# Four column groups instead of two for a one-row output on TensorE, with two casts and a store from four partitions

## The chip, the cores and the metric

The kernel runs on one core of a Trainium2 chip. The metric is the device time of one execution in microseconds (us). The five runs of the kernel before agree within 0.12%. A profile covers one execution; its span, from the first to the last instruction, is about 1.8 us shorter than the time in the kernel before. Engines: PE is TensorE (PEld its weight loads), DVE is VectorE, ACT is ScalarE, SP issues the loads and the store. PSUM is the memory in which PE sums up its products. The granted clock is the share of full speed that the profile shows for PE: 1.00 is called full clock here, 0.50 half clock.

## The reference, cut to what matters

One token of 576 numbers goes through windowed attention over a key and value cache (32 query heads, 16 key and value heads, the last 4096 positions) and through a two-layer GELU network. A gate mixes the two.

```python
x = A_x                                               # [1, 1, 576]
g = _sigmoid((x * gate_w).sum(-1, keepdims=True))
a = _A_ref(x, A_k_cache, A_v_cache, A_wq, A_wo)       # ... attention, then o @ wo, wo is [4096, 576]
b = _B_ref(x, B_w1, B_b1, B_w2, B_b2)                 # gelu(x @ w1 + b1) @ w2 + b2, w2 is [4608, 576]
return g * a + (1 - g) * b
```

Nearly all the work is reading 53.6 MB of caches and weights once. The output is a single row of 576 numbers. It is the sum of 68 products of a 128-vector with a 128 x 576 block: 36 blocks of w2, 32 of wo, all added up in PSUM. The gate is already in the vectors.

## The kernel before: the parts that matter

The row is kept as two halves of 288 columns, on PSUM partitions 0 and 32 and in different banks. Every block takes two matmuls with one stationary column each.

```python
    y_ps = ps_y.tile([64, 1024], FP32, name="y_ps")
    y_out = (y_ps[0:1, 0:DH], y_ps[32:33, 512 : 512 + DH])      # DH = 288

    def y_add(vec, row, start=False, stop=False):
        for s in range(2):
            nc.tensor.matmul(y_out[s], lhsT=vec, rhs=row[:, s * DH : (s + 1) * DH],
                             start=start, stop=stop, skip_group_check=True)
```

`y_add` is used in the middle of the kernel (first half of w2, 18 blocks) and at its end (32 blocks of wo, 18 of w2), in the order in which the last loads land. Loads are all issued by SP, far ahead of their use.

```python
    for r0, r1 in ((0, 16), (16, RO)):                           # RO = 32
        nc.sync.dma_start(out=wo_t[:, r0:r1, :], in_=wo_src[:, r0:r1, :])
    for j0, j1 in ((0, 10), (10, 16), (16, 18)):                 # the last three loads
        nc.sync.dma_start(out=w2_t[:, NJ + j0 : NJ + j1, :], in_=w2_src[:, 1, j0:j1, :])
    # ... (attention output to ov) ...
    for r in range(RO):
        y_add(ov[:, r : r + 1], wo_t[:, r, :])
    for f in range(NJ, NF):
        y_add(gt[:, f : f + 1], w2_t[:, f, :], stop=(f == NF - 1))
    out_row = const.tile([1, D], BF16, name="out_row")
    nc.scalar.copy(out=out_row[:, DH:D], in_=y_out[1])
    nc.vector.tensor_copy(out=out_row[:, 0:DH], in_=y_out[0])
    nc.sync.dma_start(out=out.rearrange("a b d -> (a b) d"), in_=out_row[:])
```

## Time and profile before

| | before |
|---|---|
| time, median of 5 runs | 134.01 us (133.95 to 134.11) |
| span of the profiled run | 132.1 us |
| 864 KB piece of w2 landed (last but one load) | 128.21 us |
| last `y_ps` matmuls | 128.25 to 129.44 us |
| casts | 129.43 to 129.88 us |
| store issued | 129.94 us |
| end | 132.1 us |

First the page of the kernel before: busy time of PE in us with its share of the span and its instructions, then the granted clock of PE and the busy share of the 16 DMA engines, in tenths, in 40 slices of the span.

```profile
PE 77.4 (59%) x1126; PEld 51.1 (39%) x1126; DVE 55.4 (42%) x80; ACT 12.9 (10%) x25; POOL 0.7 (1%) x6
...
PEclk9999999999999999999999996555555555556998
DMA  7999998999999999999999999999999999999960
```

The DMA engines are busy nearly to the end and PE is not: the loads bound the kernel. PE's clock falls to half near 80 us and comes back in the last tenth of the span.

The end of the chain of waits, before (start, length, what):

```profile
100.84 27.37 DMA w_t<-in_B_w_dram
128.21 0.04 issue
128.25 1.19 PE y_ps L193 x16
129.44 0.44 DVE out_row L437
```

After the landing at 128.21 us only the last matmuls, a cast and the store remain. The chain names the 864 KB piece; the very last one, 288 KB for two blocks, landed at 128.94 us by its semaphore, while PE was at work on the other six.

Instructions of the kernel before in order of time (start, length, engine, line, what, count, and in brackets the wait before):

```profile
72.97 1.14 PE L193 MATMUL y_ps<-w_t,gt 128*1 128x288 bf16 x15
...
117.16 4.00 PE L193 MATMUL y_ps<-wo_t,ov 128*1 128x288 bf16 x32 [3.04 <-DMA wo_t<-in_A_wo_dram]
...
122.67 2.12 PE L193 MATMUL y_ps<-wo_t,ov 128*1 128x288 bf16 x32 [1.51 <-DMA wo_t<-in_A_wo_dram]
...
128.25 1.15 PE L193 MATMUL y_ps<-w_t,gt 128*1 128x288 bf16 x16 [0.73 <-DMA w_t<-in_B_w_dram]
...
129.43 0.45 DVE L437 CAST out_row<-y_ps 1x288 bf16<-1x288 f32 x1 [15.09 <-PE y_ps L193]
129.46 0.39 ACT L436 CAST out_row<-y_ps 1x288 bf16<-1x288 f32 x1 [42.24 <-PE y_ps L193]
129.94 0.31 SPq L438 DMA_DIRECT2D out_dram<-out_row  x1
```

The groups at 117.16 and 122.67 have the same 32 matmuls, 4.00 us at half clock and 2.12 us at full clock. The casts on DVE and ACT run side by side.

The stretches of the same run (us, then busy time of PE, PEld, DVE, ACT and POOL, granted clock, DMA share, GB/s):

```profile
117.00:119.00 2.00, 1.84 (x16) 1.00 (x17) 0.00 (x0) 0.00 (x0) 0.00 (x0) 0.50 0.97 415
128.20:129.40 1.20, 1.15 (x16) 0.62 (x15) 0.00 (x0) 0.00 (x0) 0.00 (x0) 1.00 0.09 27
```

The clock is 0.50 at 117 us and 1.00 in the tail.

And the DMA queues in the stretch 117.0 to 127.8 us (queue and kind, then packets, MB and the share of the 16 engines' time):

```profile
q1 hardware_dynamic: 492, 4.24, 93.7%
```

In the last 11 us of the load stage there is one queue only, that of the loads.

### The profile page before, as it was taken

The page shows a single profiled execution, that of the slowest core. Times are in us where ns is not written, and L with a number is a line of the kernel's source. Part 1 is how long each engine was busy: PE and PEld are TensorE (multiplying, and loading weights), DVE is VectorE, ACT ScalarE, POOL GpSimd, SP SyncE. Part 2 cuts the span into 40 slices and gives each one's busy share as a digit, 9 for nine tenths or more (in the row PEclk, how much of TensorE's full clock was granted, in tenths as well). Part 3 has the DMA queues.
Part 4 walks back from the last instruction along what each step waited for, and adds up shares of the span by engine and source line. Part 5 has one row for each costly group of instructions (what it writes and reads, how often), then busy time and mean ns, then how long its engine had stood idle before and what let it go on. Part 6 is the DMA issues. An engine that isn't in the chain of part 4 may idle for free.

```text
span 132.1 us, 2458 instructions
## 1 busy us (share of the span) xinstructions
PE 77.4 (59%) x1126; PEld 51.1 (39%) x1126; DVE 55.4 (42%) x80; ACT 12.9 (10%) x25; POOL 0.7 (1%) x6
## 2 busy tenths in 40 slices
PE   0038999084699769769779460007942952456651
PEld 0035999084234323223223230007942952333430
DVE  6059100503978988988985710653000000100001
ACT  3000000003000000000000059940000000000001
POOL 2000000000000000000000000000000000000000
PEclk9999999999999999999999996555555555556998
DMA  7999998999999999999999999999999999999960
GB/s 246 421 443 411 448 518 368 398 427 427 427 417 432 422 431 419 427 436 417 454 408 442 451 446 417 407 466 427 397 451 387 431 417 428 429 407 427 406 249 0
DMA packets 3190, 53.78 MB, mean 407 GB/s; under 512 B 358, under 2 KB 362, under 8 KB 620
## 3 DMA queue, kind: packets, MB, share of 16 engines
q1 hardware_dynamic: 3170, 53.61, 95.7%
q8 instruction: 9, 0.15, 0.4%
q10 hardware_dynamic: 10, 0.01, 0.0%
q14 instruction: 1, 0.01, 0.0%
HBM read 53.62 MB, written 0.00 MB: 406 GB/s over the span
## 4 chain that ended last, share of the span: by engine, by line
DMA 67%; PE 12%; DVE 8%; ACT 7%; issue 2%; SPq 1%; DVEq 0%
DMA k_t<-in_A_k_cache_dram 26%; DMA w_t<-in_B_w_dram 21%; DMA wq_t<-in_A_wq_dram 20%; ACT p_t L351 7%; PE o_ps L402 5%; DVE kt L300 3%; PE q_ps L257 3%; DVE pt L359 2%; DVE m L321 2%; PE s_ps L309 1%; PE y_ps L193 1%; SPq L415 1%; PE t_ps L377 0%; DVE out_row L437 0%; SPq L417 0%
## 5 line engine op out<-in xcount | busy, mean ns | idle before, releaser
L300 DVE STREAM_TRANSPOSE kt<-k_t 128x2048 f32<-128x2048 f32 x16 | 36.0, 2290 | 9.7 <-DMA k_t<-in_A_k_cache_dram 9.7
L309 PE MATMUL s_ps<-kt,qz_flat 128*128 128x512 bf16 x128 | 32.3, 399 | 9.2 <-DVE kt L300 9.2
L309 PEld LDWEIGHTS <-qz_flat 128*128 128x128 bf16 x128 | 12.8, 100 | 28.3 <-issue 14.7
L402 PE MATMUL o_ps<-pt,v_t 128*128 128x8 bf16 x512 | 14.6, 168 | 8.5 <-DMA v_t<-in_A_v_cache_dram 6.5
L402 PEld LDWEIGHTS <-v_t 128*128 128x128 bf16 x512 | 14.3, 104 | 8.9 <-DMA v_t<-in_A_v_cache_dram 6.7
L351 ACT ACTIVATE p_t<-s_ps,negm 128x512 bf16<-128x512 f32 x8 | 9.7, 1412 | 44.9 <-DVE negm L342 44.9
L219 PE MATMUL h_ps<-x,w_t 128*128 128x2 bf16 x162 | 10.2, 202 | 0.0
L219 PEld LDWEIGHTS <-w_t 128*128 128x128 bf16 x162 | 10.1, 169 | 0.0
L420 DVE TENSOR_TENSOR om<-o_ps,rgh 128x128 bf16<-128x128 f32 x1 | 0.3, 292 | 22.2 <-PE o_ps L402 22.2
L193 PE MATMUL y_ps<-wo_t,ov 128*1 128x288 bf16 x64 | 6.1, 364 | 4.6 <-DMA wo_t<-in_A_wo_dram 4.6
L359 DVE STREAM_TRANSPOSE pt<-p_t 128x2048 bf16<-128x2048 bf16 x2 | 4.6, 2312 | 7.4 <-ACT p_t L351 7.4
L377 PE MATMUL t_ps<-ls,ones 128*128 128x32 f32 x2 | 0.6, 396 | 11.9 <-DVE ls L375 11.9
L193 PE MATMUL y_ps<-w_t,gt 128*1 128x288 bf16 x72 | 5.6, 285 | 2.1 <-DMA w_t<-in_B_w_dram 2.1
L437 DVE CAST out_row<-y_ps 1x288 bf16<-1x288 f32 x1 | 0.4, 446 | 15.1 <-PE y_ps L193 15.1
L257 PE MATMUL q_ps<-x,wq_t 128*128 128x2 bf16 x144 | 4.0, 166 | 4.0 <-DMA wq_t<-in_A_wq_dram 4.0
L193 PEld LDWEIGHTS <-ov 128*1 128x1 bf16 x64 | 3.4, 103 | 7.0 <-issue 4.5
L257 PEld LDWEIGHTS <-wq_t 128*128 128x128 bf16 x144 | 3.9, 104 | 4.0 <-DMA wq_t<-in_A_wq_dram 4.0
L377 PEld LDWEIGHTS t_ps<-ls,ones 128*128 128x128 f32 x2 | 0.5, 310 | 12.2 <-issue 12.2
L120 PE MATMUL xs_ps<-one_b,rows 1*128 1x1 bf16 x9 | 0.7, 195 | 7.2 <-DVE rows L117 7.2
L193 PEld LDWEIGHTS <-gt 128*1 128x1 bf16 x72 | 3.2, 83 | 3.9 <-issue 2.9
L436 ACT CAST out_row<-y_ps 1x288 bf16<-1x288 f32 x1 | 0.4, 390 | 42.2 <-PE y_ps L193 42.2
L228 DVE COPY hacc<-h_ps 128x36 f32<-128x36 f32 x1 | 0.2, 196 | 9.4 <-PE h_ps L219 9.4
(68 smaller groups left out, 28.7 us busy)
## 6 DMA issues: line engine op xcount, KB each, us to landing
k_t<-in_A_k_cache_dram SPq DMA_DIRECT2D x8, 2048.0 KB, 32.3
v_t<-in_A_v_cache_dram SPq DMA_DIRECT2D x3, 4096.0 KB, 29.8
wq_t<-in_A_wq_dram SPq DMA_DIRECT2D x1, 4608.0 KB, 25.8
wo_t<-in_A_wo_dram SPq DMA_DIRECT2D x2, 2304.0 KB, 20.2
v_t<-in_A_v_cache_dram SPq DMA_DIRECT2D x2, 2048.0 KB
w_t<-in_B_w_dram SPq DMA_DIRECT2D x1, 2880.0 KB, 14.1
w_t<-in_B_w_dram SPq DMA_DIRECT2D x1, 2592.0 KB, 11.3
w_t<-in_B_w_dram SPq DMA_DIRECT2D x1, 2304.0 KB, 8.0
```

What stands on the lines that cost most here:

```text
L120: nc.tensor.matmul(xs_ps[:, i : i + 1], lhsT=xdup[:, i : 2 * D : NI], rhs=one_b[0:1, 0:1], start=(i == 0), stop=(i == NI - 1), skip_group_ ...
L193: nc.tensor.matmul(y_out[s], lhsT=vec, rhs=row[:, s * DH : (s + 1) * DH], start=start, stop=stop, skip_group_check=True,)
L219: nc.tensor.matmul(h_ps[:, j:NF:NJ], lhsT=w1_t[:, i, j:FH:NJ], rhs=x2[:, i, :], start=False, stop=(i == NI - 1 and j == NJ - 1), skip_grou ...
L257: nc.tensor.matmul(q_ps[:, j : Hq : Hq // 2], lhsT=wq_t[:, i, j * Dh : (j + 1) * Dh], rhs=x2[:, i, :], start=(i == 0 and j == 0), stop=(i ...
L300: nc.vector.transpose(out=kt[:, u * half : (u + 1) * half].bitcast(FP32), in_=k_t[:, f, u * SL // 2 : (u + 1) * SL // 2, :] .rearrange("p ...
L309: nc.tensor.matmul(s_ps[:, u * 512 : (u + 1) * 512].rearrange("p (c k) -> p c k", k=32), lhsT=qz[:, h0 // 2, j, :], rhs=kv[:, u * SL // 4 ...
L321: nc.vector.reduce_max(out=m2[:], in_=s_ps[:].rearrange("p (n b) -> p b n", b=2), axis=AX.X)
L351: nc.scalar.activation(out=p_t[:, cs, :, b], in_=s_ps[:].rearrange("p (c k u b) -> p u b c k", k=8, u=2, b=2)[:, f, b % 2], func=ACT.Exp, ...
L359: nc.vector.transpose(out=pt[:, cs, :].rearrange("p c h -> p (c h)"), in_=p_t[:, cs, :, :].rearrange("p c k b -> p (c k b)"),)
L377: nc.tensor.matmul(t_ps[:], lhsT=ones[:], rhs=ls[:], start=True, stop=True)
L402: nc.tensor.matmul(o_ps[:, 8 * g : 8 * g + 8, 0], lhsT=v_t[:, c, :], rhs=pt[:, c, 8 * g : 8 * g + 8], start=(c == 0), stop=(c == NCK - 1),)
L415: nc.sync.dma_start(out=wo_t[:, r0:r1, :], in_=wo_src[:, r0:r1, :])
```

## The change

The row becomes four column groups of 144 on partitions 0, 32, 64 and 96 of one PSUM bank, so that four quarters of PE's array should work at a time. Two engines cast 64 partitions each, and the store takes four pieces of 288 bytes. The intent was to shorten the matmuls and the casts after the last load.

```diff
-    y_ps = ps_y.tile([64, 1024], FP32, name="y_ps")
-    y_out = (y_ps[0:1, 0:DH], y_ps[32:33, 512 : 512 + DH])
-    def y_add(vec, row, start=False, stop=False):
-        for s in range(2):
+    DQ = D // 4
+    y_ps = ps_y.tile([P, DQ], FP32, name="y_ps")
+    def y_add(vec, row, m=1, start=False, stop=False):
+        for s in range(4):
             nc.tensor.matmul(
-                y_out[s],
+                y_ps[32 * s : 32 * s + m, :],
                 lhsT=vec,
-                rhs=row[:, s * DH : (s + 1) * DH],
+                rhs=row[:, s * DQ : (s + 1) * DQ],
                 start=start, stop=stop,
+                tile_position=(0, 32 * s),
                 skip_group_check=True,
             )
-    y_add(ones[0:1, 0:1], b2g[0:1, :], start=True)
+    y_add(ones[0:1, 0:32], b2g[0:1, :], m=32, start=True)
 ... (nothing else until the end)
-    out_row = const.tile([1, D], BF16, name="out_row")
-    nc.scalar.copy(out=out_row[:, DH:D], in_=y_out[1])
-    nc.vector.tensor_copy(out=out_row[:, 0:DH], in_=y_out[0])
-    nc.sync.dma_start(out=out.rearrange("a b d -> (a b) d"), in_=out_row[:])
+    y_sb = const.tile([P, DQ], BF16, name="y_sb")
+    nc.scalar.copy(out=y_sb[64:P, :], in_=y_ps[64:P, :])
+    nc.vector.tensor_copy(out=y_sb[0:64, :], in_=y_ps[0:64, :])
+    nc.sync.dma_start(
+        out=out.rearrange("a b (s n) -> (a b s) n", s=4),
+        in_=y_sb[:].rearrange("(s l) n -> s l n", l=32)[:, 0, :],
+    )
```

## The prediction

> **What bounds the kernel now.** Its loads. The queue table gives the load queue 95.7% of the 16 DMA engines' span; in the slices the DMA stays near nine tenths, mean 407 GB/s for 53.6 MB. PE is busy 59%, DVE 42%. The chain listed in order of time ends so: the last weights land at 128.21 us, 16 y_ps matmuls run 128.25 to 129.44, the DVE cast takes 0.44 us (446 ns; the ACT cast, 390 ns, runs beside it), the rest up to 132.1 is the store and the end. So only some 3.9 us after the last landing can change, unless a buffer release that the loads wait for is delayed.
>
> **What the change touches.**
> 1. Matmuls onto y_ps. Each vector takes four column groups of 144 instead of two of 288; matmuls and weight loads double. The two groups already ran side by side: the timeline has 32 matmuls in 2.12 us at full clock, 59 ns each after the last one's own 0.28 us, while 288 columns alone would take 120 ns (estimate from the Trainium skill, "TensorE: Matmul & The Clock Gate", Back-to-back issue gap). At half clock it is 114 ns each. Four side by side would halve a vector's array time, 118 to 60 ns at full clock. But short load-and-matmul pairs cost 28 to 29 ns at either clock (q_ps 144 in 4.0 us, o_ps 64 in 1.87 us); four are 112 ns. So issue should eat the gain at full clock (118 to 112 ns) and leave one at half clock (228 to 120 ns), in hidden stages. The tail of 8 vectors, 32 pairs: 31 x 28 ns + 0.23 us = 1.1 us against 1.15 us.
> 2. Clock. The windows view shows 0.50 up to 120 us, 1.00 from 121.2, after 4 us of dense wo matmuls. Those will take about 2 us, so PE looks less busy and the clock may not come back before the tail, which then takes about 1.35 us. I give that 45%.
> 3. Casts. DVE from PSUM takes 192 ns for 32 columns and 446 for 288, about 1 ns a column, so 144 take about 300 ns: 0.14 us saved on the chain. ACT falls to about 270 ns. They read different partitions, after the matmuls.
> 4. Store. Four pieces of 288 B instead of one of 1152 B: 0 to 0.1 us more.
> 5. Earlier. The y_ps matmuls near 73 to 78 us surround the softmax maximum chain; the instruction order has 22 of them between mt_ps and mb_ps instead of 10: 0.6 us against 0.86 us, so no delay. The loads are saturated there, so tenths are hidden.
>
> **Sum.** Matmul tail -0.05 (clock kept) or +0.2 (lost), cast -0.14, store +0.05: -0.15 to +0.1 us, all on the critical path and all about 0.1% of the time. Predicted 133.9 us, 133.4 to 134.3 holding 8 times in 10 (repeats of before spread 0.16 us). Faster by over 2%: 1%; within: 98%; slower: 1%.
>
> **What would show it.** Step 1: y_ps groups after 128 us; starts 28 ns apart confirm issue as the limit, 15 ns full overlap and a tail of 0.7 us. Step 2: granted clock from 121 us. Step 3: the casts' durations. Step 4: time from the store's issue to the end. Step 5: DMA slices unchanged, last landing within 0.3 us of 128.2.
>
> **What would make it wrong.** Column groups that do not overlap when four share one bank (32 x 60 ns, +0.9 us); a store much slower in small pieces (+0.5 us); a moved last landing from a shifted load schedule. All stay within 2%.

## The result, and the profile after

| | before | after | difference |
|---|---|---|---|
| time, median of 5 runs each | 134.01 us | 136.15 us (135.74 to 136.49) | +2.14 |
| span of the profiled run | 132.1 us | 134.0 us | +1.9 |
| 864 KB piece of w2 landed | 128.21 us | 129.52 us | +1.31 |
| from there to the end of the matmuls | 1.23 us | 1.21 us | -0.02 |
| from there to the store's issue | 0.50 us | 0.65 us | +0.15 |
| from there to the end of the span | 2.20 us | 2.65 us | +0.45 |

The ratio of the times is 1.0158, with a 95% interval of 1.0137 to 1.0178. Ratios here are the mean time of one kernel's runs over that of the other's of the same rounds, so they are not quite the ratio of the medians. The change is a loss of 1.6%: still "within 2%", but far outside the predicted range of 133.4 to 134.3 us.

The same views after the change. The page:

```profile
PE 74.3 (55%) x1266; PEld 52.0 (39%) x1266; DVE 55.2 (41%) x80; ACT 12.8 (10%) x25; POOL 0.7 (1%) x6
...
PEclk9999999999999999999999855555555555555555
DMA  7999998999999999999999999999999999999910
```

The clock stays at half to the end. The DMA is as busy as before, a little longer.

The end of the chain:

```profile
100.52 29.00 DMA w_t<-in_B_w_dram
129.52 0.04 issue
129.56 1.17 PE y_ps L193 x32
130.75 0.28 ACT y_sb L437
131.06 0.30 DVE y_sb L438
```

The landing moved from 128.21 to 129.52 us, and there are two casts in a row now, where one stood.

In order of time:

```profile
72.77 0.72 PE L193 MATMUL y_ps<-w_t,gt 128*1 128x144 bf16 x33
...
117.11 2.09 PE L193 MATMUL y_ps<-wo_t,ov 128*1 128x144 bf16 x64 [3.04 <-DMA wo_t<-in_A_wo_dram]
...
123.96 2.09 PE L193 MATMUL y_ps<-wo_t,ov 128*1 128x144 bf16 x64 [4.75 <-DMA wo_t<-in_A_wo_dram]
...
129.56 1.14 PE L193 MATMUL y_ps<-w_t,gt 128*1 128x144 bf16 x32 [0.74 <-DMA w_t<-in_B_w_dram]
...
130.75 0.27 ACT L437 CAST y_sb<-y_ps 64x144 bf16<-64x144 f32 x1 [43.52 <-PE y_ps L193]
131.06 0.30 DVE L438 CAST y_sb<-y_ps 64x144 bf16<-64x144 f32 x1 [16.75 <-ACT y_sb L437]
131.38 0.65 SPq L439 DMA_DIRECT2D out_dram<-y_sb  x1
```

Four readings. The matmuls did get faster: 64 of half the width take 2.09 us where 32 took 4.00 us, both at half clock. The second chunk of wo starts at 123.96 instead of 122.67 us: the loads were already late by 1.3 us there, while the first chunk (117.11) was not late at all. DVE waits for ACT's cast. And the issue of the store takes 0.65 us instead of 0.31.

The stretches:

```profile
117.00:119.00 2.00, 1.89 (x64) 1.88 (x64) 0.00 (x0) 0.00 (x0) 0.00 (x0) 0.50 0.99 424
129.50:130.70 1.20, 1.14 (x32) 0.78 (x31) 0.00 (x0) 0.00 (x0) 0.00 (x0) 0.50 0.02 6
```

The clock is 0.50 in the tail. Yet 32 matmuls in the tail take 1.14 us, the time of 16 before at full clock.

The queues in 117.0 to 127.8 us:

```profile
q1 hardware_dynamic: 490, 4.24, 93.9%
q8 instruction: 1, 0.02, 0.6%
```

One packet of queue q8, kind "instruction", is new in this stretch. The packet list of the trace has it at 121.23 us, 16384 bytes, 1.07 us long. The Trainium skill ("Runtime: NRT & Kernel Launch", Instruction fetch mechanics) says that an engine's instruction memory is refilled in 16 KiB blocks of 256 instructions, which its sequencer fetches through a DMA queue of its own. The trace agrees with the size: 16384 bytes, in queue q8. Before the change eight such blocks began inside the load stage and the ninth at 128.21 us; after it the ninth began at 121.23 us.

The landings show whom it hurt. Each load is split over 16 DMA engines, and each of them raises the load's semaphore once when its share has landed (the Trainium skill, "DMA: Bandwidth & Descriptors", Why a DMA increments its semaphore by 16 and not by 1; the trace has 16 landings for every large load). One engine's share of the loads is called a ring here. These are the 16 landing times in us of the second chunk of wo, sorted, from the semaphore records of the trace:

```
before  120.82 120.82 120.83 120.91 120.96 121.06 121.13 | 121.76 | 122.22 122.28 122.33 122.34 122.50 122.53 122.58 122.62
after   120.49 120.75 120.90 120.91 120.97 121.00 121.04 | 121.66 | 122.16 122.24 122.32 122.36 122.42 122.43 122.58 | 123.92
```

Fifteen rings are as early as before. One is 1.33 us behind the next, and a load is complete only when its last ring is. In the kernel before, seven rings are on time, one is half late and eight are late, by 1.5 us on the mean, and it fetched eight blocks in the load stage. After the change seven are late once and one is late twice, with nine blocks. No load was issued late: SP issued the 864 KB piece at 100.52 us, and at 100.84 us before the change.

So the theory R: a block of PE instructions rides on one of the 16 load rings (it goes through the same DMA engine) and sets it back by about 1.3 to 1.5 us; the first eight blocks fall on eight different rings, the ninth on one that was hit already, and the last ring decides. What moved the landing is then not what the four groups do, but how many instructions they take. Rival L: the groups themselves, their place in PSUM or the lost clock delay the landing. Rival S: every block costs the loads as a whole 1.3 us.

### The profile page after: what moved, and what is told of

It reads as the page before. It is cut to its first block, busy times and chain, and to the rows that moved or that the text cites. A ratio compares the mean times of both kernels' runs of the same rounds, so it can differ in the third digit from the quotient of the medians. Undisturbed runs are those within 1.5% of the kernel's fastest.

```text
span 134.0 us, 2738 instructions
## 1 busy us (share of the span) xinstructions
PE 74.3 (55%) x1266; PEld 52.0 (39%) x1266; DVE 55.2 (41%) x80; ACT 12.8 (10%) x25; POOL 0.7 (1%) x6
## 4 chain that ended last, share of the span: by engine, by line
DMA 67%; PE 12%; DVE 8%; ACT 8%; issue 2%; SPq 1%; DVEq 0%
DMA k_t<-in_A_k_cache_dram 26%; DMA w_t<-in_B_w_dram 22%; DMA wq_t<-in_A_wq_dram 19%; ACT p_t L352 7%; PE o_ps L403 5%; DVE kt L301 3%; PE q_ps L258 3%; DVE pt L360 2%; DVE m L322 2%; PE s_ps L310 1%; PE y_ps L193 1%; SPq L416 1%; PE t_ps L378 0%; PE mb_ps L339 0%; SPq L418 0%
## 5 line engine op out<-in xcount | busy, mean ns | idle before, releaser
L193 PE MATMUL y_ps<-wo_t,ov 128*1 128x144 bf16 x128 | 4.2, 323 | 7.8 <-DMA wo_t<-in_A_wo_dram 7.8
L193 PE MATMUL y_ps<-w_t,gt 128*1 128x144 bf16 x144 | 4.7, 282 | 2.1 <-DMA w_t<-in_B_w_dram 2.1
```

The source lines that it names most:

```text
L193: nc.tensor.matmul(y_ps[32 * s : 32 * s + m, :], lhsT=vec, rhs=row[:, s * DQ : (s + 1) * DQ], start=start, stop=stop, tile_position=(0, 32 ...
```

## The experiments

Twelve kernels had a run: the changed one and the eleven below. Times are medians; "before" was run in the same rounds each time (134.02, 134.07 and 134.13 us in the three sets). In the second set three of the eleven runs of before took 134.87 to 135.21 us, so ratios of that set are a little low.

### More PE instructions in the kernel before

Nothing but dummy work is added to the kernel before. The result stays correct, the row stays in two groups.

```diff
+    pad_ps = ps_m.tile([1, 2], FP32, name="pad_ps", tag="m")
 ... (at the end of each of the 8 K blocks; N = 1, 4, 16, 32 for pad16, pad64, pad256, pad512)
+            for _ in range(N):
+                nc.tensor.matmul(
+                    pad_ps[:, 0:2], lhsT=ident[:, 0:1], rhs=ident[:, 0:2], start=True, stop=True
+                )
```

pad64, as expected:

> The kernel before plus 64 PE instructions (4 pairs of a weight load and a tiny matmul after each of the 8 K blocks, where PE waits anyway; output correct, y_ps in two groups as before). Theory R (a 16 KB block of PE instructions, fetched inside the load stage, delays one of the 16 load rings by 1.3 us; the ninth block falls on a ring that already carried one): PE reaches the ninth block's boundary 64 instructions earlier, the block is fetched near 125 us instead of 128.2, one ring finishes about 1.3 us after the other fifteen, last landing about 129.4 us, time about 135.2 us. Rival L (the four column groups themselves, their place in PSUM, or the lost clock delay the landing): 134.0 us, landing 128.2 us.

Measured: 135.36 us, ratio 1.0097 (1.0082 to 1.0112). Last landing of the 864 KB piece 129.40 us. Its ninth block began at 126.60 us. From the end of its chain, and from its queues in 117.0 to 127.8 us:

```profile
100.83 28.57 DMA w_t<-in_B_w_dram
q8 instruction: 1, 0.02, 0.6%
```

pad256:

> The kernel before plus 256 hidden PE instructions, about as many as the change adds (272). Theory R: nine blocks inside the load stage as in the changed kernel, one ring hit twice, last landing about 129.5 us, time about 135.3 us (134.0 + 1.3). Rival L: 134.0 us.

Measured: 135.31 us, ratio 1.0096; landing 129.59 us. Four times as many instructions cost the same. These two runs speak against rival L: neither the groups nor the store were touched, and the landing is late all the same. The clock in the tail was 1.00 in pad64, so a lost clock is not needed either. That four groups alone do not delay the landing is shown by cut216 below.

pad16:

> The kernel before plus only 16 hidden PE instructions. Theory R: the ninth boundary lies somewhere in the last 72 instructions; if 16 do not carry it into the chunk of work before 126 us the time stays 134.0 us; if they do, it jumps by the full 1.3 us to 135.3. A time in between, near 134.1, would speak for a cost in proportion to the instructions.

Measured: 134.08 us, ratio 1.0006 (0.9991 to 1.0021); landing 128.18 us, ninth block at 128.40 us. So the cost is a step between 16 and 64 instructions and not in proportion to them.

pad512:

> The kernel before plus 512 hidden PE instructions: ten blocks inside the load stage. Theory R, where the last ring decides and the tenth block falls on a second ring: two rings finish last together, time stays about 135.3 us as with 256. Rival S (every block costs the loads as a whole 1.3 us): 136.6 us. Rival L: 134.0 us.

Measured: 137.56 us, ratio 1.028. This is none of the expected values, and the time does not decide. The stretch of 62 to 75 us shows why, pad512 first, then the kernel before (us, busy time of PE, PEld, DVE, ACT, POOL, clock, DMA share, GB/s):

```profile
62.00:75.00 13.00, 11.21 (x49) 4.52 (x47) 12.32 (x6) 0.00 (x0) 0.00 (x0) 1.00 0.88 352
```

```profile
62.00:75.00 13.00, 9.88 (x53) 4.05 (x51) 10.62 (x5) 0.00 (x0) 0.00 (x0) 1.00 1.02 434
```

PE has more to do there, and the DMA share fell from 1.02 to 0.88: the loads ran dry. The buffers of K came free late: SP issued the next load at 65.57 us instead of 61.30, and its list of waits puts 8.6 us before that load down to DVE's transposes of K, against 4.5 us before. That is another loss, and not the one in question. Its landings fit theory R if the stall let the rings catch up: five of the ten blocks began after it, and of the 864 KB piece eleven rings landed by 129.97 us and five from 130.97 to 131.74 us.

padx512 puts the same 512 instructions where PE waits for the exponentials:

```diff
     for f in range(NJ):
         y_add(gt[:, f : f + 1], w2_t[:, f, :])
+    pad_ps = ps_m.tile([1, 2], FP32, name="pad_ps", tag="m")
+    for _ in range(256):
+        nc.tensor.matmul(
+            pad_ps[:, 0:2], lhsT=ident[:, 0:1], rhs=ident[:, 0:2], start=True, stop=True
+        )
```

> The kernel before plus 512 hidden PE instructions again, now all of them in the 12 us in which PE waits for the exponentials, because in the K stage they slowed PE itself and the loads ran dry. Theory R (the last ring decides; the tenth block falls on another ring): two rings finish last, 135.3 us. Rival S (each further block costs 1.3 us): 136.6 us. If the loads do not run dry this is the clean test of the two.

Measured: 135.48 us, ratio 1.0084. The end of its chain:

```profile
102.02 27.72 DMA w_t<-in_B_w_dram
129.74 0.04 issue
```

Two more blocks than before came in the load stage, and the landing is at 129.74 us: 1.5 us late and not 2.6. Two rings are late twice, at 129.51 and 129.74 us. This is what theory R expects, and rival S falls.

### Fewer PE instructions

cut216 is the changed kernel with 216 PE instructions left out (the first half of w2, the b1 terms and one of nine slices of w1). Every load stays.

```diff
-    for j in range(NJ):
-        nc.tensor.matmul(h_ps[:, j:NF:NJ], lhsT=b1_t[:, j:FH:NJ], rhs=ident[0:2, 0:2], ...)
-    for i in range(NI):
+    for i in range(NI - 1):
         for j in range(NJ):
             nc.tensor.matmul(h_ps[:, j:NF:NJ], lhsT=w1_t[:, i, j:FH:NJ], rhs=x2[:, i, :], ...)
 ...
-    for f in range(NJ):
-        y_add(gt[:, f : f + 1], w2_t[:, f, :])
```

> The changed kernel (four groups, its casts and store) minus 216 PE instructions: the w2 first half, the b1 terms and one of nine w1 slices are left out, so the result is wrong on purpose; all loads stay. Theory R: the ninth block is fetched after the loads again, last landing back at about 128.2 us, time about 134.85 us (136.15 - 1.3), the rest of the loss (serial casts, store of four pieces) remains. Rival L (four groups delay the landing): stays at 136.1 us with landing near 129.5 us.

Measured: 134.55 us, ratio 1.0044 (1.0029 to 1.0059); landing 128.25 us. With four groups kept and the instructions gone, 1.6 us of the loss is gone too, 1.27 us of it in the landing. What remains, 0.5 us, is about what the cast and the store cost (0.15 and 0.45 us above). The end of its chain begins so:

```profile
102.37 25.88 DMA w_t<-in_B_w_dram
```

cutb takes 288 PE instructions out of the kernel before (the same cut, with five of nine slices of w1).

```diff
-    for i in range(NI):
+    for i in range(NI - 5):
 ... (b1 terms and first half of w2 left out as in cut216)
```

> The kernel before minus 288 PE instructions (w2 first half, b1 terms and five of nine w1 slices left out; wrong on purpose; all loads stay): one block fewer, seven inside the load stage. Theory R (the last ring decides): seven rings are hit once instead of eight, the last one as late as ever, 134.0 us. Rival S (each block costs the loads as a whole): 132.7 us.

Measured: 134.45 us, ratio 1.0022 (0.9978 to 1.0067), from runs of 133.87, 134.02, 134.88 and 135.02 us. Seven blocks began in the load stage, and the landing is at 128.19 us, as with eight. So fewer blocks do not help as long as one ring is hit once, again as theory R has it; rival S wanted 132.7. The split of the four runs has another cause, which the profile caught, as it was taken of the run of 134.88 us. Its tail matmuls, in order of time, and then the stretch from 128.2 to 129.4 us:

```profile
128.23 2.08 PE L193 MATMUL y_ps<-w_t,gt 128*1 128x288 bf16 x16 [0.73 <-DMA w_t<-in_B_w_dram]
```

```profile
128.20:129.40 1.20, 1.17 (x12) 0.64 (x13) 0.00 (x0) 0.00 (x0) 0.00 (x0) 0.53 0.05 17
```

In this run the clock had fallen back to half at the start of the tail, and 16 matmuls in two groups took 2.08 us instead of 1.15. Two groups pay 0.9 us for that; the four groups of the changed kernel at the same half clock took 1.14 us. The three long runs of before in the second set look the same in size, but none of them was profiled, so that is argued only.

All landings of the 864 KB piece in one table, without pad512 and ring11, whose loads ran otherwise. A ring is on time up to 127.05 us, half late from 127.1 to 127.5, late once from 127.75 to 128.45, late twice from 129.4; blocks are those that began before 127.8 us. PE instructions are counted as they were added or cut, the 280 of the change by its trace.

| kernel | PE instructions against before | blocks | on time / half late / late once / late twice | last ring, us |
|---|---|---|---|---|
| cutb | -288 | 7 | 7 / 2 / 7 / 0 | 128.19 |
| before | 0 | 8 | 7 / 1 / 8 / 0 | 128.21 |
| pad16 | +16 | 8 | 7 / 1 / 8 / 0 | 128.18 |
| cut216 | +64 | 8 | 7 / 1 / 8 / 0 | 128.25 |
| cutrow | +64 | 8 | 7 / 1 / 8 / 0 | 128.22 |
| pad64 | +64 | 9 | 7 / 1 / 7 / 1 | 129.40 |
| pad256 | +256 | 9 | 7 / 1 / 7 / 1 | 129.59 |
| after | +280 | 9 | 7 / 1 / 7 / 1 | 129.52 |
| onedve | +280 | 9 | 7 / 1 / 7 / 1 | 129.61 |
| onerow | +280 | 9 | 7 / 1 / 7 / 1 | 129.78 |
| padx512 | +512 | 10 | 7 / 1 / 6 / 2 | 129.74 |

In every row the blocks equal the rings late once plus twice those late twice. (cut216 has more instructions than before in all, but its last 18 blocks alone take 144 against 72; ahead of them PE has run 2172 by the trace, against 2180 in the kernel before. cutrow, onedve and onerow are described below.) The landings of the earlier loads fit in time as well: pad64 has no ring late twice in the load that ended at 126.29 us, its ninth block began at 126.60 us, and in the next load there is one. In cut216 and cutrow only seven rings are late in the second chunk of wo; the eighth block began at 121.02 and 120.75 us, while that chunk was landing, and in the next load eight are late. The half-late ring may be the one that carried an 8 KB instruction packet near 51 us, which all these runs have; that was not tested.

### The cast and the store

onedve replaces the two casts by one:

```diff
-    nc.scalar.copy(out=y_sb[64:P, :], in_=y_ps[64:P, :])
-    nc.vector.tensor_copy(out=y_sb[0:64, :], in_=y_ps[0:64, :])
+    nc.vector.tensor_copy(out=y_sb[:], in_=y_ps[:])
```

> The changed kernel with one DVE cast of all 128 partitions in place of the ACT cast and the DVE cast that waited for it. If the serial pair is what the tail lost there: from the end of the matmuls to the store's issue about 0.35 us instead of 0.67, time about 135.85 us (136.15 - 0.3). If the cast order does not matter: 136.15 us. The landing of the last weights stays near 129.5 us either way.

Measured: 135.75 us, ratio 1.0107 (1.0074 to 1.0140). The tail:

```profile
130.84 0.31 DVE L437 CAST y_sb<-y_ps 128x144 bf16<-128x144 f32 x1 [16.49 <-PE y_ps L193]
131.18 0.65 SPq L438 DMA_DIRECT2D out_dram<-y_sb  x1
```

One DVE cast of 128 partitions takes 0.31 us, as long as one of 64 (0.30). From the end of the matmuls to the issue of the store it is now 0.35 us instead of 0.65. The serial pair cost 0.3 us against this, and 0.15 us against the parallel pair of the kernel before. DVE's wait for ACT is in the built program: the instruction list of the changed kernel has it, though the two casts share no partition. In variants that were only built and not run it stayed with two banks in one tile, and went when each half of the row had a PSUM tile of its own.

onerow casts four quarters into one row and stores it whole:

```diff
-    y_ps = ps_y.tile([P, DQ], FP32, name="y_ps")
+    y_ps = ps_y.tile([P, 1024], FP32, name="y_ps")
 ...
-                y_ps[32 * s : 32 * s + m, :],
+                y_ps[32 * s : 32 * s + m, 512 * (s // 2) : 512 * (s // 2) + DQ],
 ...
+    out_row = const.tile([1, D], BF16, name="out_row")
+    for q in range(2):
+        nc.scalar.copy(out=out_row[:, (2 + q) * DQ : (3 + q) * DQ],
+                       in_=y_ps[64 + 32 * q : 65 + 32 * q, 512 : 512 + DQ])
+        nc.vector.tensor_copy(out=out_row[:, q * DQ : (q + 1) * DQ], in_=y_ps[32 * q : 32 * q + 1, 0:DQ])
+    nc.sync.dma_start(out=out.rearrange("a b d -> (a b) d"), in_=out_row[:])
```

> The changed kernel with the four groups in two banks, cast by four short casts (two on ACT, two on DVE, side by side) into one row, which is stored in one piece as before. If the four-piece store costs 0.5 us: time from the store's issue to the end about 2.15 us instead of 2.6, store's issue 0.31 us instead of 0.65, and about 135.65 us in all. If the store of four pieces costs nothing and the 0.5 us is chance: 136.1 us. Landing near 129.5 us.

Measured: 135.72 us, ratio 1.0105 (1.0071 to 1.0139). The tail:

```profile
131.00 0.61 DVE L442 CAST out_row<-y_ps 1x144 bf16<-1x144 f32 x2 [16.64 <-PE y_ps L193]
131.04 0.56 ACT L438 CAST out_row<-y_ps 1x144 bf16<-1x144 f32 x2 [43.59 <-PE y_ps L193]
131.67 0.31 SPq L445 DMA_DIRECT2D out_dram<-out_row  x1
```

The issue takes 0.31 us again, and from the issue to the end of the span it is 2.27 us; with four pieces it was 2.65 us in the changed kernel and 2.71 us in onedve. So four pieces cost 0.4 to 0.5 us, of which 0.34 us is the longer issue. The matmuls of the tail take the same 1.14 us in two banks as in one.

cutrow is onerow with the cut of cut216: all three losses removed.

> The changed kernel with all three suspected losses taken out: 216 PE instructions fewer (wrong on purpose), four short casts side by side into one row, store in one piece. If late ring, serial casts and four-piece store are the whole loss: 134.1 us (134.55 of the same cut without the new casts and store, minus 0.4), the same as before. If something else of the four groups costs: still 134.5 us or more.

Measured: 134.35 us (134.05 to 134.39), ratio 1.0021 (1.0004 to 1.0038). That is 0.2 us above before and 1.8 us below the changed kernel. Its span was 132.5 us against 132.1. The three causes explain the loss but for this rest, and the rest sits in the tail: the matmuls ended 1.39 us after the landing at 128.22 instead of 1.23 (at half clock, and the last piece landed at 129.11 us), and two casts in a row on each engine take 0.61 us for what took 0.45.

### An attempt to use the finding

ring11 tries to spare some rings by loading the last 288 KB of the kernel before as 88 and 40 partitions:

```diff
-    for j0, j1 in ((0, 10), (10, 16), (16, 18)):
+    for j0, j1 in ((0, 10), (10, 16)):
         nc.sync.dma_start(out=w2_t[:, NJ + j0 : NJ + j1, :], in_=w2_src[:, 1, j0:j1, :])
+    for p0, p1 in ((0, 88), (88, P)):
+        nc.sync.dma_start(out=w2_t[p0:p1, NJ + 16 : NF, :], in_=w2_src[p0:p1, 1, 16:NJ, :])
```

> The kernel before with the last 288 KB of w2 loaded as 88 and 40 partitions instead of 128, by the Trainium skill's rule (DMA: Bandwidth & Descriptors, how many engines) on rings 0 to 10 and 0 to 9: rings 11 to 15 carry 18 KB less, the others up to 9 KB more. If the eight rings that carry instruction blocks are among the high ones, some of the lag of 1.3 us is taken back: about 133.6 us. If they are the low ones, they get later: about 134.4 us. It tells which rings are hit, and whether moving load bytes off them pays.

Measured: 135.06 us, ratio 1.0071 (1.0021 to 1.0122). A miss. The two loads landed on 11 and on 10 rings as expected, but among the eleven four were late and one half late; that leaves four late ones among the other five rings, so the late rings lie on both sides and this split cannot spare them. Why the late rings also brought the 864 KB piece 0.8 us later (129.08 us) is not known. No version was found that beats the kernel before.

## Why the prediction was wrong

- **Bound by the loads: right.** The DMA is busy to the end in both kernels.
- **"Only some 3.9 us after the last landing can change, unless a buffer release that the loads wait for is delayed": this step failed.** The last landing moved by 1.31 us, from 128.21 to 129.52, where the prediction's own test asked for 0.3 us at most; and the last loads were issued no later than before. What moved it was left out of the sum: 280 more PE instructions bring one more 16 KB block into the load stage, and the ring that finishes last is then late twice. Adding 64 instructions to the kernel before does the same (135.36 us), and cutting 216 from the changed kernel undoes it (landing 128.25 us). The prediction named "a moved last landing from a shifted load schedule" as a risk, but gave it no size, and the load schedule was not the cause.
- **Step 1, issue limits four groups to 112 ns a vector at full clock: wrong, in the kernel's favour.** Near 73 us, at full clock, 33 matmuls take 0.72 us: their starts are 15.5 ns apart on average, 62 ns a vector, against 122 ns before. The starts in the tail show it at half clock, in us, from the trace:

```
before (full clock)  128.25 128.26 | 128.37 128.38 | 128.50 128.50 | 128.62 128.62 ...
after (half clock)   129.56 129.56 129.57 129.57 | 129.64 129.64 129.64 129.64 | 129.76 129.76 129.76 129.76 | 129.88 ...
```

  Four start within 0.01 us, and the next four 0.12 us later. So the four groups do run side by side, as the Trainium skill has it ("TensorEngine Tiling (Array Packing)", Key Properties: tiles operate independently), and the issue is not the limit: a vector takes 62 ns at full clock and 120 ns at half, where the prediction had the issue cost the same at either clock. The rate of 28 ns was taken from groups of another kind (128-column weights), and it did not carry over.
- **Step 2, the clock may not come back: it did not.** It was 0.50 to the end. The cost was mis-sized: 1.14 us in the tail, not 1.35, since at half clock the four groups still manage a vector in 0.12 us. The gain of the four groups was thus real, and used up in making good the lost clock. That 1.14 us lies near the 1.1 us forecast for a kept clock is luck: the clock was lost and the groups overlapped more than forecast, and the two cancel.
- **Step 3, casts: durations right, arrangement wrong.** They took 0.30 and 0.27 us as forecast, but one after the other. Instead of 0.14 us saved it was 0.15 us lost.
- **Step 4, store: mis-sized.** 0 to 0.1 us was said, it was 0.45. The prediction named "a store much slower in small pieces (+0.5 us)" as a risk, but left it out of the sum.
- **Step 5, no delay near the softmax maximum: right.** The exponentials start at 77.57 us instead of 77.56.

The sum for the spans: 1.31 - 0.02 + 0.15 + 0.45 = 1.89 us, which is the 1.9 us between 132.1 and 134.0. The remaining 0.25 us of the 2.14 us between the medians lies outside the span: time less span was 1.83 to 2.49 us in the five runs of the changed kernel, 1.8 us in the profiled run of before. Its cause stays open.

What is shown and what is not: that the number of PE instructions moves the landing, in one step and with the number of blocks, is shown by the runs. Which ring carries which block is not recorded; that it is the late ring rests on the counts in the table and on the times at which the late rings appear. Why a block of 1.07 us sets its ring back by 1.3 to 1.5 us was not found out, nor why the ninth block falls on a ring that was hit already.

## What to carry to other kernels

In a kernel bound by loads to the very end, count the instructions of the busiest engine as well as its time: each further 16 KB block can set back one DMA ring, the last ring decides, and an edit that doubles many small matmuls may cost more there than it saves on PE. Look for it in the landings of the last loads, ring by ring, and pad the old kernel with hidden instructions to test it. In a tail of 4 us, the pieces of the store (0.45 us) and the wait between two casts (0.15 us) weighed more than what the matmuls gained (0.02 us).

## What the Trainium skill lacked or had wrong

- "Runtime: NRT & Kernel Launch", Instruction fetch mechanics, calls the cost of crossing a 16 KiB boundary "mostly hidden". Here one crossing more cost 1.3 us (pad64: 135.36 us against 134.02), and it was not PE that waited: the last load landed 1.2 us later, on one ring of 16. That the fetch of a block can delay loads is on no page.
- "TensorE: Matmul & The Clock Gate" gives about 25 ns as the least distance from start to start, in Part 1 and without an exception. In four column groups it was 15.5 ns on average at full clock, and four starts fell within 10 ns. The page's own Part 3, on packed matmuls, has starts about 4 ns apart, so the floor should be limited to matmuls that are not packed.
- "DMA: Bandwidth & Descriptors" asks for 512 bytes or more in a transfer, but has no figure for what the number of pieces adds to the issue and the end of a tiny last store. Four pieces of 288 bytes instead of one of 1152 cost 0.45 us, of which 0.34 us was SP's issue (0.65 against 0.31 us).
